# q and the gate operand transposed by DMA, x2 in row tiles of 128, column tiles and a new tail in an attention and convolution-gate kernel

## Chip, cores, metric

The kernel runs on one core of one Trainium2 chip. The metric is device time in microseconds (us) of one execution. A profile is one execution taken by the hardware profiler. Its engines are TensorE (PE for matmuls, PEld for weight loads), VectorE (DVE), ScalarE (ACT), GpSimd (POOL) and SyncE (SP), which in this kernel only issues DMAs. An eviction is the copy of a matmul result out of PSUM, where the matmuls of the kernel put it. A landing is the time from the issue of a DMA until its data have arrived.

## The reference

B = 8 batches, 8 heads, S = 576 positions, head width 64, model width DM = 512; all inputs fp32.

```python
# phi(x) = concat(relu(x)*cos, relu(x)*sin), cos and sin of pi/2 * position / S
q_p, k_p = phi(q), phi(k)
kv  = einsum('bhsf,bhsd->bhfd', k_p, v)
z   = sum(k_p, axis=s)
x   = einsum('bhsf,bhfd->bhsd', q_p, kv) / (einsum('bhsf,bhf->bhs', q_p, z) + 1e-6)
x   = heads side by side                                   # B, S, DM
x1, x2, x3 = split(x @ w_proj, 3)
x2_conv = irfft(rfft(x2, axis=s) * rfft(filter, axis=s))   # along the 576 positions
out = (x1 * x2_conv * x3) @ w_out                          # fp32
```

## The kernel before

One batch goes through `phi` (VectorE), `qt` (q transposed), `kv`, `num` and `att` (attention), `fx` (a fold of the positions that also transposes), `x2` and `dft` (forward transform), the gate (x1, x3, `g`), `inv` (inverse transform), `y` and `out`. Stages of three batches are interleaved by a scheduler. The parts that matter here, with cuts marked:

```python
qpt_buf = [consts.tile([128, NH, NT, 2, 64], FP16, ...) for i in range(1)]     # one buffer

def emit_qt(b, hp):                    # q is transposed by TensorE
    u = psum.tile([128, 2, 1024], FP16, ...)
    for hh in range(2):
        for j in range(NJ):
            nc.tensor.transpose(u[:, hh, ds(j * NP, NP)],
                                qp[:, j, 2 * hp + hh].rearrange("p a b -> p (a b)"), perm)
    ...                                # two evictions to qpt, VectorE and ScalarE

def emit_num(b, hp):
    ...                                # reads qpt as weights: the first reader of the transposed q

def emit_x2(b, bls):                   # 24 matmuls of 96 rows
    for bl in bls:
        for comp in range(2):
            for c in range(NC):
                nc.tensor.matmul(u[0:NP, comp], fx[:, c, ds(comp * 6 + 2 * bl, 2)]...,
                                 wp16[:, c, ds(DM, DM)], start=(c == 0), stop=(c == NC - 1))
        ...

OT = [0, 128, 256, 384, 448]
def emit_out(b, grps):
    ov = out[b].rearrange("(p j) n -> j p n", j=6)         # rows j, j+6, j+12, ... of the output
    for grp in grps:
        ...                                                # matmuls, eviction to os_
        for t in grp:
            ...                                            # pieces x..e of at most 96 rows
            src = os_[x - OT[t] : e - OT[t], t - grp[0]]
            dst = ov[jb, p_a:p_b]                          # 96 x 512: outermost count 96
            q_ = nc.scalar if b >= B - 2 and t % 2 == 1 else nc.sync
            q_.dma_start(out=dst, in_=src)
```

Of the kernel before, what the change touches and what calls it, by code (L numbers as in the profile page):

```python
# [17 lines left out]
def kernel(  # L18
# [15 lines left out]

    nc = tc.nc
# [6 lines left out]
    NT = 5  # L42
# [25 lines left out]
    tcol = consts.tile([128, NJ], FP32, tag="tcol", name="tcol")  # L68
    epsc = consts.tile([128, NT], FP32, tag="epsc", name="epsc")
    perm = consts.tile([NP, NP], FP16, tag="perm", name="perm")  # L70
# [5 lines left out]
    fm = consts.tile([128, 24, 10], FP16, tag="fm", name="fm")  # L76
    tre = consts.tile([NP, 3, NP], FP16, tag="tre", name="tre")
    tim = consts.tile([NP, 3, NP], FP16, tag="tim", name="tim")

# [9 lines left out]
    qpt_buf = [consts.tile([128, NH, NT, 2, 64], FP16, tag=f"qpt{i}", name=f"qpt{i}") for i in range(1)]  # L89
# [24 lines left out]
    raw_t = {}  # L114

    def load_qk(b, nm, hs=slice(0, NH)):
        src = {"q": q, "k": k, "v": v}[nm]
        if hs.start == 0:
            rw = work.tile([NP, NH, NJ * D], FP16, tag="raw", bufs=4, name=f"{nm}raw{b}")
            raw_t[(b, nm)] = rw  # L120
        nc.gpsimd.dma_start(
            out=raw_t[(b, nm)][:, hs], in_=src[b, hs].rearrange("h (p j) d -> p h (j d)", j=NJ)
        )

    def emit_va(b, xs=range(4)):
        for x in xs:
            hs = slice(2 * x, 2 * x + 2)
            nc.scalar.copy(  # L128
                out=va_buf[b % 2][:, hs, :, 0:D],
                in_=raw_t[(b, "v")][:, hs].rearrange("p h (j d) -> p h j d", j=NJ),  # L130
            )
# [28 lines left out]
    def emit_iotas(part):  # L160
# [13 lines left out]
        iota("sr_i", [NP, QS], lambda t: [(t, [[2, 3], [12, NP // 2]], 1, 0)])  # L174

    def emit_cols():
# [6 lines left out]
        nc.vector.memset(warm, 0.0)  # L183
        sj = cc["s6_i"]
# [3 lines left out]
        nc.vector.tensor_tensor(out=tcol, in0=tcol, in1=scol, op=AL.mult)  # L188

        u16 = small("u16p")  # L190
        rnd(u16, p, 1.0 / 16.0, -15.0 / 32.0)
        dest = small("dest")
        tsc(dest, p, 6.0, AL.mult)
        nc.vector.scalar_tensor_tensor(
            out=dest, in0=u16, scalar=-95.0, in1=dest, op0=AL.mult, op1=AL.add
        )
        tsc(perm, cc["nrow_i"], dest[0:NP], AL.is_equal)

    def emit_pads():
        for va in va_buf:  # L200
            nc.vector.memset(va[:, :, :, D : D + 2], 1.0 / A1)
        for t in qpt_buf:
            nc.vector.memset(t[:, :, :, 0, 60:64], 0.0)
            nc.vector.memset(t[:, :, :, 1, 0:4], 0.0)

    def emit_fm():

        p = cc["p"]
        loc = small("loc")
        side = small("side")  # L210
        nc.vector.tensor_copy(out=loc[0:64], in_=p[0:64])
        tsc(loc[64:128], p[64:128], -1.0, AL.mult, 127.0, AL.add)
        nc.vector.memset(side[0:64], 1.0)
        nc.vector.memset(side[64:128], -1.0)
        lo = small("lo")
        rnd(lo, loc, 1.0 / 6.0, -5.0 / 12.0)
        li = small("li")
        nc.vector.scalar_tensor_tensor(
            out=li, in0=lo, scalar=-6.0, in1=loc, op0=AL.mult, op1=AL.add
        )  # L220


        orb = small("orb", NT)
        for t in range(NT):
            tsc(orb[:, t : t + 1], lo, 10.0 * t, AL.add)
        oj = small("oj", NT)
        rnd(oj, orb, 1.0 / 16.0, -15.0 / 32.0)
        pos = small("pos", NT)

        tsc(pos, orb, 6.0, AL.mult)  # L230
        nc.vector.scalar_tensor_tensor(
            out=pos, in0=oj, scalar=-95.0, in1=pos, op0=AL.mult, op1=AL.add
        )
        nc.vector.scalar_tensor_tensor(
            out=pos, in0=li.to_broadcast([128, NT]), scalar=96.0, in1=pos, op0=AL.mult, op1=AL.add
        )
# [6 lines left out]
        orow_i = cc["orow_i"][:, 0:10]  # L243
        match = small("match", 10)
# [5 lines left out]
        for sl, (kk, c0) in enumerate([(0, 0.25), (3, 0.25), (1, 0.25), (1, 0.0), (2, 0.25), (2, 0.0)]):  # L250
# [4 lines left out]
        nc.scalar.activation(out=coef[:, 0:6], in_=ph, func=AF.Sin, scale=TWO_PI)  # L255
        tsc(coef[:, 3:6:2], coef[:, 3:6:2], 1.0 / R3, AL.mult)

        tsc(coef[:, 0:6], coef[:, 0:6], 2.0, AL.mult)
        tsc(coef[:, 0:6], coef[:, 0:6], RC, AL.add, -RC, AL.add)
        tsc(coef[:, 0:6], coef[:, 0:6], 0.5, AL.mult)  # L260
        tsc(coef[:, 6:12], coef[:, 0:6], side, AL.mult)
# [12 lines left out]
            in0=coef.unsqueeze(2).to_broadcast([128, 24, 10]),  # L274
            in1=match.unsqueeze(1).to_broadcast([128, 24, 10]),
# [23 lines left out]
    def emit_rows():  # L299
# [5 lines left out]
        par = cc["par"] = small("par")  # L305
        rnd(par, p, 0.5, -0.25)
        nc.vector.scalar_tensor_tensor(
            out=par, in0=par, scalar=-2.0, in1=p, op0=AL.mult, op1=AL.add
        )
# [10 lines left out]
    def emit_fwd_tables():  # L320
# [4 lines left out]
        u = small("u16")  # L325
        rnd(u, p, 1.0 / 16.0, -15.0 / 32.0)
        j = small("jr")
        nc.vector.scalar_tensor_tensor(
            out=j, in0=half, scalar=-3.0, in1=u, op0=AL.mult, op1=AL.add
        )  # L330
        w = small("w2s")

        tsc(w, p, 12.0, AL.mult, 1.0, AL.add)
        nc.vector.scalar_tensor_tensor(out=w, in0=u, scalar=-192.0, in1=w, op0=AL.mult, op1=AL.add)
        nc.vector.scalar_tensor_tensor(out=w, in0=j, scalar=2.0, in1=w, op0=AL.mult, op1=AL.add)
# [24 lines left out]
        for tb in (tre, tim):  # L360
            tsc(tb[:, 1:3], tb[:, 1:3], amp[0:NP], AL.mult)
            nc.vector.tensor_tensor(out=tb[:, 0], in0=tb[:, 0], in1=mask, op=AL.mult)

# [59 lines left out]
    def emit_h():  # L423
        hc, hs_, hb, alt = cc["hc"], cc["hs"], cc["hb"], cc["alt"]
        fa = filt16.rearrange("p x (j n) -> p x j n", j=3)
        for x, op in ((0, AL.add), (1, AL.subtract)):
# [5 lines left out]
        for bl in range(3):  # L432
# [15 lines left out]
            tsc(h3[:, bl, 1], u[0:NP, 1], sc, AL.mult)  # L448
            nc.vector.tensor_copy(out=h3[:, bl, 2], in_=h3[:, bl, 1])
        u = unit("h_nyq")  # L450
        for j in range(3):
            nc.tensor.matmul(
                u[0:1, 0], alt[:, j % 2 : j % 2 + 1], feo[:, 0, j], start=(j == 0), stop=(j == 2)
            )
        nc.scalar.activation(out=h3[0:1, 0, 2], in_=u[0:1, 0], func=AF.Copy, scale=1.0 / S)
# [4 lines left out]
    def emit_phi(b, nm, h0=0, nh=NH):  # L460
        rw = raw_t[(b, nm)]
        dst = kp_t if nm == "k" else qp_t
        if h0 == 0:
            dst[b] = work.tile([NP, NJ, NH, 2, D], FP16, tag=f"{nm}p", bufs=2 if nm == "q" else 1, name=f"{nm}p{b}")
        t = dst[b]
        if nm == "q":

            tsc(
                t[:, :, h0 : h0 + nh, 0],
                rw[:, h0 : h0 + nh].rearrange("p h (j d) -> p j h d", j=NJ), 0.0, AL.max,  # L470
            )
        for j in range(NJ):
            for cs, col in ((0, ccol), (1, scol)) if nm == "k" else ((1, tcol),):
                mark["phi", b, nm] = tsc(
                    t[:, j, h0 : h0 + nh, cs], rw[:, h0 : h0 + nh, ds(j * D, D)],
                    col[0:NP, j : j + 1], AL.mult, 0.0, AL.max,
                )
# [21 lines left out]
    def emit_qt(b, hp):  # L499
        qp, qpt = qp_t[b], qpt_buf[0]  # L500
        u = psum.tile([128, 2, 1024], FP16, tag="u", bufs=4, name=f"qt{b}_{hp}")
        for hh in range(2):
            for j in range(NJ):
                nc.tensor.transpose(  # L504
                    u[:, hh, ds(j * NP, NP)],
                    qp[:, j, 2 * hp + hh].rearrange("p a b -> p (a b)"),
                    perm,
                )
        hsl = slice(2 * hp, 2 * hp + 2)
        ev = nc.scalar.copy if b == 0 and hp < 2 else nc.vector.tensor_copy  # L510
        mark["qpt", b, hp] = ev(  # L511
            out=qpt[:, hsl, :, 0, 0:60],
            in_=u[:, :, 0:300].rearrange("p h (t c) -> p h t c", c=60),
        )
        nc.scalar.copy(  # L515
            out=qpt[:, hsl, ::-1, 1, 4:64],
            in_=u[:, :, 276:576].rearrange("p h (t c) -> p h t c", c=60),
        )

    def emit_num(b, hp, wm=0):  # L520
        qpt, kvs = qpt_buf[0], kvs_t[b]
        if hp == 0:
            att_t[b] = work.tile([128, NT, DM], FP16, tag="att", bufs=2, name=f"att{b}")
# [3 lines left out]
        for hh in range(2):  # L527
            h = 2 * hp + hh
            for t in range(NT):
                nc.tensor.matmul(  # L530
                    u[:, hh, ds(t * 65, 65)], qpt[:, h, t].rearrange("p a b -> p (a b)"),
                    kvs[:, h // 4, ds((h % 4) * 65, 65)], start=True, stop=True,
                )
        nv = u[:, :, 0 : NT * 65].rearrange("p h (t e) -> p h t e", e=65)
        rcp = work.tile([128, 2, NT], FP32, tag="rcp", bufs=2, name=f"rcp{b}_{hp}")
        nc.vector.tensor_tensor(
            out=rcp, in0=nv[:, :, :, 64], in1=epsc.unsqueeze(1).to_broadcast([128, 2, NT]), op=AL.add
# [5 lines left out]
            in1=rcp.unsqueeze(3).to_broadcast([128, 2, NT, D]),  # L543
# [3 lines left out]
    def emit_fx(b, cs=range(NC), ccs=None, wm=0):  # L547
        att = att_t[b]
        if 0 in cs:
            fx_t[b] = work.tile([128, NC, 24, 48], FP16, tag="fx", bufs=2, name=f"fx{b}")  # L550
        fx = fx_t[b]
        for c in cs:
            u = unit(f"fx{b}_{c}")
            warm_up(u, wm)
            for t in range(NT - 1):
                nc.tensor.matmul(  # L556
                    u[:, t // 2, 0:480].rearrange("p (g o) -> p g o", o=20)[:, :, ds((t % 2) * 10, 10)],
                    att[:, t, ds(c * 128, 128)], fm, start=True, stop=True,
                )
            nc.scalar.copy(  # L560
# [319 lines left out]
```

## Time and profile before

| | before |
|---|---|
| time, median of 3 runs | 270.46 us (270.35 to 270.78) |
| TensorE busy | 243.0 us, 90% of the span |
| steady period per batch | 28.5 us, of it TensorE 27.9 |
| last 13.6 us | output evictions wait for stores |

The prediction below shows and reads the main views. Two lines more: TensorE's busy share in 40 slices of the span (each digit in tenths), and the issue line of the large output stores, whose last number is the median from issue to landing.

```profile
PE   0287998878989999999999999999999999999991
...
out_dram<-os SPq DMA_DIRECT2D x22, 192.0 KB, 2.5
```

Each digit is the mean busy share of the core's 16 DMA engines in 0.3 us.

```profile
DMA  0000000000289899965891039956779453799971
```

### The profile page before, as it was taken

To read this page: it belongs to the slowest core of one execution; us is meant where nothing else is said; L and a number is where in the kernel's file an instruction comes from. 1 tells how busy PE (TensorE), PEld (TensorE's weight loads), DVE (VectorE), ACT (ScalarE), POOL (GpSimd) and SP (SyncE) were. 2 spreads that over 40 slices of the span, in tenths; PEclk is the share of its full clock that TensorE was granted. 3 is DMA by queue.
4 is the path that set the end of the run, shared out by engine and by line. 5 is a ranking of instruction groups with operands and counts; after the bars stand their busy time and mean duration, and the time that the engine had idled before them with its cause. 6 is when DMAs were issued, how large, how long until landed. Compare 5 with 4: busy or idle time off the path is not lost.

```text
span 271.2 us, 6320 instructions
## 1 busy us (share of the span) xinstructions
PE 243.0 (90%) x2457; PEld 175.2 (65%) x2457; DVE 226.9 (84%) x805; ACT 196.8 (73%) x274; POOL 27.3 (10%) x47
## 2 busy tenths in 40 slices
PE   0287998878989999999999999999999999999991
PEld 0164767547858776786678676867687768756830
DVE  7689997998899898979897989978997479646951
ACT  2279679798497778877897789786977667857630
POOL 8551111020020101110111011000000000000000
PEclk9999999995799999999999999999999999999998
DMA  5999998919019296636860868114000600060235
GB/s 79 168 206 205 206 205 122 166 14 169 3 14 161 33 230 90 89 40 152 150 101 3 174 128 124 16 51 125 0 2 9 169 2 0 2 174 13 69 117 155
DMA packets 26991, 26.70 MB, mean 98 GB/s; under 512 B 1680, under 2 KB 22160, under 8 KB 26960
## 3 DMA queue, kind: packets, MB, share of 16 engines
q0 software_dynamic: 21200, 16.84, 42.7%
q1 hardware_dynamic: 5120, 8.39, 10.7%
q10 hardware_dynamic: 640, 1.05, 1.3%
q8 instruction: 19, 0.31, 0.5%
q14 instruction: 12, 0.10, 0.1%
HBM read 33.69 MB, written 9.44 MB: 159 GB/s over the span
## 4 chain that ended last, share of the span: by engine, by line
PE 50%; ACT 22%; DVE 21%; DMA 4%; issue 1%; POOL 0%; SPq 0%; POOLq 0%; ACTq 0%
PE x L630 20%; PE x L593 9%; ACT x2f L598 7%; ACT va L128 7%; PE kv L491 5%; PE out L695 4%; PE fx L556 4%; DVE eo L672 4%; ACT fx L560 3%; DMA vraw<-in_v_dram 2%; DVE kp L99 2%; PE qt L504 2%; PE dft L607 2%; PE inv L657 2%; DVE qpt L511 2%; PE inv L656 2%
## 5 line engine op out<-in xcount | busy, mean ns | idle before, releaser
L630 PE MATMUL x<-fx,wp 128*128 128x288 f16 x512 | 67.5, 286 | 1.1 <-ACT fx L560 1.0
L630 PEld LDWEIGHTS <-wp 128*128 128x128 f16 x512 | 50.0, 98 | 13.3 <-issue 0.3
L593 PE MATMUL x<-wp,fx 128*96 128x512 f16 x192 | 45.2, 382 | 0.5 <-ACT x2f L598 0.5
L560 ACT CAST fx<-fx 128x960 f16<-128x960 f32 x32 | 30.6, 961 | 13.7 <-PE fx L556 13.7
L695 PE MATMUL out<-wo,y 128*128 128x512 f16 x160 | 37.6, 379 | 0.7 <-DVE y L677 0.7
L598 ACT ACTIVATE x2f<-x 96x1024 f16<-96x1024 f32 x24 | 24.5, 1020 | 14.6 <-PE x L593 14.6
L593 PEld LDWEIGHTS <-fx 128*96 128x96 f16 x192 | 22.4, 124 | 15.1 <-issue 0.8
L672 DVE TENSOR_TENSOR eo<-eq 128x144 f16<-128x144 f16 x128 | 23.7, 228 | 10.1 <-ACT eq L660 9.9
L128 ACT COPY va<-vraw 96x768 f16<-96x768 f16 x32 | 25.3, 827 | 9.3 <-DMA vraw<-in_v_dram 9.3
L638 DVE TENSOR_TENSOR g<-x,x1s 128x288 f16<-128x288 f32 x64 | 27.0, 448 | 1.3 <-PE x L630 1.1
L491 PE MATMUL kv<-va,kp 96*128 96x65 f16 x384 | 16.4, 202 | 11.7 <-ACT va L128 8.8
L540 DVE TENSOR_TENSOR att<-num,rcp 128x640 f16<-128x640 f32 x32 | 26.1, 820 | 0.3
L515 ACT COPY qpt<-qt 128x600 f16<-128x600 f16 x32 | 20.4, 671 | 7.5 <-DVE qpt L511 7.5
L695 PEld LDWEIGHTS <-y 128*128 128x128 f16 x160 | 14.9, 97 | 16.0 <-DVE y L677 1.2
L609 ACT CAST xf<-dft 96x1024 f16<-96x1024 f32 x24 | 23.5, 1010 | 2.2 <-PE dft L607 1.2
L491 PEld LDWEIGHTS <-kp 96*128 96x128 f16 x384 | 15.3, 104 | 13.3 <-DVE kp L99 8.1
L504 PEld LDWEIGHTS <-qp 96*128 96x128 f16 x384 | 20.2, 102 | 5.1 <-issue 1.1
L636 ACT CAST x1s<-x 128x576 f16<-128x576 f32 x32 | 20.5, 639 | 4.2 <-PE x L630 3.1
L612 DVE TENSOR_TENSOR m<-xf,h 96x1024 f16<-96x1024 f16 x24 | 16.3, 678 | 7.8 <-ACT xf L609 7.7
L504 PE MATMUL qt<-perm,qp 96*128 96x96 f16 x384 | 21.7, 213 | 0.5 <-ACT fx L560 0.3
L700 ACT ACTIVATE os<-out 128x1024 f32<-128x1024 f32 (+1 forms) x21 | 18.3, 883 | 5.2 <-PE out L695 5.1
L556 PE MATMUL fx<-fm,att 128*128 128x240 f16 x128 | 18.8, 270 | 2.2 <-DVE att L540 1.1
(185 smaller groups left out, 419.4 us busy)
## 6 DMA issues: line engine op xcount, KB each, us to landing
out_dram<-os SPq DMA_DIRECT2D x22, 192.0 KB, 2.5
qraw<-in_q_dram POOLq DMA_DIRECT2D x7, 576.0 KB, 6.6
kraw<-in_k_dram POOLq DMA_DIRECT2D x7, 576.0 KB, 6.3
vraw<-in_v_dram POOLq DMA_DIRECT2D x7, 576.0 KB, 6.5
out_dram<-os SPq DMA_DIRECT2D x20, 128.0 KB, 2.4
wp<-in_moe_w_proj_dram POOLq DMA_DIRECT2D x3, 512.0 KB, 12.3
out_dram<-os SPq DMA_DIRECT2D x22, 64.0 KB, 2.1
kraw<-in_k_dram POOLq DMA_DIRECT2D x2, 288.0 KB, 6.4
```

Of the source, the lines that this page charges most:

```text
L128: nc.scalar.copy(out=va_buf[b % 2][:, hs, :, 0:D], in_=raw_t[(b, "v")][:, hs].rearrange("p h (j d) -> p h j d", j=NJ),)
L491: nc.tensor.matmul(u[:, h // 4, ds((h % 4) * 65, 65)], kp[:, j, h].rearrange("p a b -> p (a b)"), va[:, h, j, 0:65], start=(j == 0), stop= ...
L504: nc.tensor.transpose(u[:, hh, ds(j * NP, NP)], qp[:, j, 2 * hp + hh].rearrange("p a b -> p (a b)"), perm,)
L540: mark["att", b, hp] = nc.vector.tensor_tensor(out=att[:, :, ds(hp * 128, 128)].rearrange("p t (h d) -> p h t d", h=2), in0=nv[:, :, :, 0: ...
L556: nc.tensor.matmul(u[:, t // 2, 0:480].rearrange("p (g o) -> p g o", o=20)[:, :, ds((t % 2) * 10, 10)], att[:, t, ds(c * 128, 128)], fm, s ...
L560: nc.scalar.copy(out=fx[:, c, :, 0:40].rearrange("p g (u o) -> p u g o", u=2), in_=u[:, :, 0:480].rearrange("p u (g o) -> p u g o", o=20),)
L593: nc.tensor.matmul(u[0:NP, comp], fx[:, c, ds(comp * 6 + 2 * bl, 2)].rearrange("p a b -> p (a b)"), wp16[:, c, ds(DM, DM)], start=(c == 0) ...
L598: mark["x2f", b, bl] = nc.scalar.mul(out=x2f[:, bl], in_=u[0:NP], mul=X2SC)
L630: nc.tensor.matmul(u[:, hf, 0:HS], wp16[:, i, ds(w * DM + c * 128, 128)], fx[:, i, ds(12 + 6 * hf, 6)].rearrange("p a b -> p (a b)"), star ...
L638: mark["g", b, c] = nc.vector.tensor_tensor(out=(g[:, c, 0:HS] if hf == 0 else g[:, c, HS:S][:, ::-1]).rearrange("p (j i o) -> p j i o", j ...
L672: nc.vector.tensor_tensor(out=eoh[:, a, :, ds(48 * x, 48)], in0=eqj[:, a, 0], in1=eqj[:, a, 1], op=op)
L695: nc.tensor.matmul(u[:, x], y[:, c, ds(OT[t], 128)], wo16[:, c], start=(c == 0), stop=(c == NC - 1),)
```

## The change

The intent: take work off TensorE, the fullest engine. q is transposed by DMA from batch 2 on; the gate operand is transposed by DMA for the last three batches instead of folded on TensorE; x2 uses full row tiles of 128, with zero-padded DFT tables to take up the shifted rows; a last tile of 64 columns goes through two column tiles; the tail is rearranged. To suit the new order of positions (pairs of blocks side by side) the output rows get a new view too. The core of the diff, with cuts marked:

```diff
+    XT_DMA = (5, 6, 7)
+    DMA_QT = 2
...                                            # emit_qt
+        if b >= DMA_QT:
+            nc.sync.dma_start_transpose(
+                out=qpt[:, hsl].rearrange("p h (j n) -> p (h j) n", j=NJ),
+                in_=qp[:, hsl].rearrange("p h j a b -> p (h j a b)"),
+            )
+            return
...                                            # emit_xt, for batches in XT_DMA
+        nc.sync.dma_start_transpose(
+            out=xt_t[b].rearrange("p t c n -> p (t c) n"),
+            in_=att_t[b].rearrange("p t n -> p (t n)"),
+        )
...                                            # emit_x2: 16 matmuls of 128 rows, then
+                for c in range(2):
+                    for x in range(2):
+                        mm(u[ds(64 * x, 64), 0], 4, 64, c + 2 * x, range(2 * x, 2 * x + 2))
...                                            # emit_gate: x3 through ScalarE to fp16
+            nc.scalar.copy(out=x3s, in_=us[1][:, :, 0:HS])
...                                            # emit_out
-    OT = [0, 128, 256, 384, 448]
+    OT = [0, 128, 256, 384, 512]
-        ov = out[b].rearrange("(p j) n -> j p n", j=6)
+        ov = out[b].rearrange("(k x y) n -> x y k n", x=2, y=6)
...
-                    dst = ov[jb, p_a:p_b]
-                    q_ = nc.scalar if b >= B - 2 and t % 2 == 1 else nc.sync
-                    q_.dma_start(out=dst, in_=src)
+                    m, k0 = pos // 48, pos % 48
+                    e = pos + 96 if pos % 96 == 0 and pos + 96 <= hi_ else min(hi_, (m + 1) * 48)
+                    q_ = nc.sync
+                    if last:
+                        q_ = (nc.sync, nc.scalar)[store[0] % 2]
+                    ...
+                    if e - pos == 96:
+                        q_.dma_start(out=ov[:, m // 2], in_=sv[pos - OT[t] : e - OT[t]])
+                    elif t < 4 or last:
+                        q_.dma_start(out=ov[m % 2, m // 2, k0 : k0 + e - pos], in_=...)
```

## The prediction

> **What bounds the kernel now.** I read the page first (busy time, slices), then the busy time by stage, then TensorE's timeline of one steady batch, then VectorE's, then the waits of the tail.
>
> ```profile
> PE 243.0 (90%) x2457; PEld 175.2 (65%) x2457; DVE 226.9 (84%) x805; ACT 196.8 (73%) x274; POOL 27.3 (10%) x47
> ...
> PEclk9999999995799999999999999999999999999998
> DMA  5999998919019296636860868114000600060235
> ```
>
> ```profile
> 50.00:71.40 21.40, 18.12 (x203) 14.00 (x202) 20.22 (x64) 16.23 (x23) 1.54 (x2) 0.77 0.64 94
> ...
> 129.30:157.80 28.50, 27.89 (x303) 20.66 (x302) 25.68 (x85) 23.03 (x31) 2.32 (x3) 1.00 0.63 113
> 157.80:186.30 28.50, 27.89 (x303) 20.67 (x302) 25.68 (x85) 23.04 (x31) 1.54 (x2) 1.00 0.46 85
> ```
>
> The columns of the stage table are span, then busy us of PE, PEld, DVE, ACT, POOL, then clock, DMA share and GB/s. After some 71 us of set-up the kernel repeats a period of 28.5 us per batch, in which TensorE is busy 27.9 us: it is the bound. VectorE (25.7) is close behind, ScalarE (23.0) less so. In the set-up VectorE is the full one, and from 61 to 71 us TensorE runs at about half clock.
>
> ```profile
> 133.81 1.90 PE L593 MATMUL x<-wp,fx 128*96 128x512 f16 x8
> ...
> 136.86 0.38 PE L607 MATMUL dft<-x2f,tre 96*96 96x512 f16 x1 [0.28 <-ACT x2f L598]
> 137.08 0.38 PE L607 MATMUL dft<-x2f,tim 96*96 96x512 f16 x1
> 137.29 2.12 PE L630 MATMUL x<-fx,wp 128*128 128x288 f16 x16
> 139.25 0.57 PE L556 MATMUL fx<-fm,att 128*128 128x240 f16 x4
> 139.66 2.12 PE L630 MATMUL x<-fx,wp 128*128 128x288 f16 x16
> ...
> 151.46 1.89 PE L695 MATMUL out<-wo,y 128*128 128x512 f16 x8
> 153.19 0.68 PE L504 MATMUL qt<-perm,qp 96*128 96x96 f16 x12
> 153.70 1.03 PE L695 MATMUL out<-wo,y 128*128 128x512 f16 x4
> ```
>
> A printed mean (286 ns for a gate matmul) is latency; what an instruction costs is the distance from start to start. From this timeline: x2 217 ns, dft 215, gate 122 (16 in 1.96 us), fx 102, its remainder fxc 82, out 215, qt 42.5 (12 in 0.51), and in the same way num 30.5, kv 32, inv 65. It is close to the number of moving columns over 2.4 per ns, whatever the height. A batch: x2 24x0.217=5.2, num 40x0.0305=1.2, dft 6x0.215=1.3, gate 64x0.1225=7.8, fx and fxc 2.0, inv 2.1, out 20x0.215=4.3, qt 48x0.0425=2.0, kv 1.5: 27.5 of the 28.5 us.
>
> ```profile
> ACT os L702 <- DMA out_dram<-os: 3.1, 2, 2.0
> DVE os L97 <- ACT os L702: 2.8, 1, 2.8
> ACT os L700 <- PE out L695: 2.0, 1, 2.0
> DVE os L97 <- DMA out_dram<-os: 1.9, 1, 1.9
> ```
>
> These are the waits of the last 13.6 us (257.6 to the end): the last output tiles wait for stores to free their buffers, two DMA landings of about 2 us in a row on the path.
>
> **What the Trainium skill says.** "DMA: Bandwidth & Descriptors", section "Latency and other measured facts", gives 261 GB/s for a DMA transpose with a non-contiguous middle dimension. The trace of before has no such transpose and can't confirm it. "TensorEngine Tiling (Array Packing)", section "Key Properties": different tiles of the array execute in parallel, and a change of tiling mode drains the array. Before has no 64-column tile, so this is untried here too. "VectorE: DVE Perf Modes", section "Walkthrough: the 8-slice pipeline in each mode": two 16-bit values per cycle need 16-bit operands of step one; fp32 or PSUM operands fall back to one. The trace agrees: 128x288 takes 448 ns with an fp32 PSUM operand (g) and 304 ns all in fp16 (y<-eo). "TensorE: Matmul & The Clock Gate", Part 1: idle windows halve TensorE's clock. It agrees: 0.50 to 0.57 from 61 to 72 us, after a stretch with gaps; inv spacing there is 120 ns instead of 65.
>
> **The change, part by part** (counts from the changed kernel's instruction lists).
>
> q transposes: the short title speaks of the gate operand, but in the code q is also transposed by DMA from batch 2 on, four DMAs a batch. Removed: 6 batches x 2.04 = 12.2 us of TensorE, and four evictions each on VectorE and ScalarE per batch.
>
> Gate operand: fx and xt are now separate folds of 24 matmuls of 96 columns each (0.0425 us, from qt's equal width): 2.04 a batch against 1.97, so +0.6 over all. For the last three batches the xt half goes: 3x1.02 = -3.1.
>
> x2: 16 matmuls of 128 rows plus four 64-column tiles. 3.5 + (0.43 if tile pairs overlap, 0.87 if not) = 3.9 to 4.3 against 5.2: -7 to -10.5 over 8 batches. In exchange dft has 9 matmuls, not 6: +0.65x8 = +5.2. num has 48, not 40: +0.24x8 = +1.9.
>
> out: the fifth tile is 64 rows in two column tiles of 256 columns: 0.43 to 0.86 against 0.86: 0 to -3 over seven batches.
>
> TensorE sum: -12.2 +0.6 -3.1 -7..-10.5 +5.2 +1.9 +0..-3 = -14.6 to -21, say -18. A steady batch with the tensor fold is then 24.7 to 25.6 us of matmul, with the DMA gate 23.7 to 24.6.
>
> VectorE per steady batch, by distances: g from 0.365 to 0.22 because x3 is copied to fp16 by ScalarE, 8x0.145=-1.2; eo 16x0.145 to 8x0.22 = -0.6; qpt 4x0.38 = -1.5; two va copies taken over from ScalarE +0.8; att with six tiles +0.5: 25.7 to about 23.8. ScalarE: +4x0.56 for x3, +0.4 for the folds, -4x0.57 qpt, -2x0.72 va, -0.4 x2f: about 21.5, and 19 with the DMA gate. Neither passes TensorE, though VectorE comes within 2 us of it.
>
> DMA: the share of 0.63 in a 28.5 us stage is 18 us. Four transposes of 96x1536 fp16 (295 KB) at the page's rate are 1.13 us each, 4.5 a batch (an estimate from that page), and q's load in halves makes more, smaller packets, perhaps +1.5. That is 24 of some 26 us: nearly full. The author's stopping at three batches for the gate operand fits this: the three last are those with the least input still to load. Since qp is made one batch ahead, a batch's transposes have about 20 us from the last read of qpt by num to their use, so latency is hidden.
>
> Tail: five single buffers instead of shared ones, evictions split over two engines, the last contraction step held back until y is whole. The two landings in a row go: from the last gate matmul to the end I expect 9.5 us (y 2.5, output matmuls 3.5, evict 0.5, issue and landing 3) instead of 13.6: -4.
>
> Set-up: x2(0) fills gaps of the set-up, so the half-clock stretch may shrink (inv's 32 matmuls lost 1.8 us and kv 1 there), but VectorE is full there and gains only about 1.5: 0 to -3.
>
> Sum: 270.5 -18 -4 -1.5 = 247. I don't take all of it: where TensorE, VectorE and ScalarE are all near 90% a period ends later than its fullest engine, today by 1 us of wait. Adding 0.6 us in each of five periods gives 250.
>
> **The rivals.**
> A. VectorE takes over. It waits 2.8 us a period today (1.8 of it for the first eq). If it keeps those waits, a period is 23.8+2.8=26.6, only 1.9 less than now; five periods give -9.5, with tail, set-up and last batches about 256. For: 84% busy over the span, against 90%. Also in the gate stage ScalarE needs 4x0.57=2.3 us per column block against TensorE's 2.5, so PSUM is freed just in time. Against: only this stage is tight for ScalarE.
> B. The transposes are several times slower than the page's rate. At 3.4 us each the DMA need is 18+1.5+13.6=33 us a batch, above the period; num would wait for qpt, stores queue behind them on the same issuing engine, and the time would be 270 to 280. For: no transpose in the trace to go by, one issuing queue. Against: the author kept four a batch and added three more.
> C. Everything is realised, tile pairs overlap and the clock dip vanishes: 242 to 244.
>
> **Range and chances.** The main sum gives 250, A 256, C 243. I centre on 250 with 241 to 260, which leaves B and worse outside. B with more than half its loss is what it takes to be within 2% or slower: faster 0.92, same 0.06, slower 0.02.
>
> **What would show it.** Right: the steady period is 25.5 to 26.5 us with TensorE still over 93% busy in it; no qt matmul after batch 1; g at about 300 ns and eo about 300; 64-column x2 tiles in pairs that start within a few ns or 217 ns apart (settles 0.43 or 0.87); DMA share near 0.9 in the middle; 9 to 10 us from last gate matmul to end, without a wait of an eviction for a store. Wrong: transposes that take over 3 us of all engines, with waits of num for qpt; VectorE without idle time while TensorE waits for g, att or y; a set-up longer than 72 us before x2 of batch 1 is done.

## The result

| | before | after |
|---|---|---|
| median | 270.4 us (270.17 to 270.78, 4 runs) | 280.87 us (279.63 to 281.85, 4 runs) |
| ratio to before | | 1.038 (95% 1.034 to 1.043): slower |
| TensorE busy | 243.0 us | 230.5 us |
| mean granted clock, profiled run | 0.978 | 0.929 |

A ratio here and below is the mean time of one kernel's fast runs over that of the other's of the same rounds, so not quite the ratio of the medians quoted. The prediction of 250 us (241 to 260) was wrong, in direction too.

TensorE did get less to do. The page's slices (TensorE, its granted clock, the DMA engines) show where the time is lost instead: in slices 22 to 24, a little at 28, at 36 and in the last three, where before was full but for the last.

```profile
PE   0379979989699999999993559998999999959600
...
PEclk9995999998999999999997579999999999988965
DMA  6999997999991978998959989897989493232330
```

The busy time by stage (columns as in the prediction) shows a period as predicted, then (one undisturbed period is left out) the disturbed one, then 14.7 us at the end in which TensorE does nothing:

```profile
95.40:120.69 25.29, 25.29 (x295) 18.16 (x293) 24.31 (x77) 20.96 (x32) 3.54 (x5) 1.00 0.92 121
...
145.98:185.00 39.02, 28.38 (x268) 18.37 (x267) 22.85 (x72) 19.20 (x28) 1.54 (x2) 0.83 1.17 141
264.40:279.10 14.70, 0.00 (x0) 0.00 (x0) 0.00 (x0) 0.38 (x1) 0.00 (x0) 0.57 0.21 54
```

The first line is what the prediction asked for: 25.29 us a period, TensorE without a gap. The chain of work that ended last, in order of time (start, us, what), names the two losses: landings of transposed q in the middle, landings of stores near the end.

```profile
144.34 1.63 PE kv L543 x48
...
146.21 17.29 DMA qpt<-qp
163.54 0.57 PE num L584 x12
...
184.01 7.21 DMA qpt<-qp
...
231.72 7.12 DMA out_dram<-os
238.86 0.62 SPq L842
239.53 8.13 DMA out_dram<-os
```

A landing on the chain is not idle time in full, since TensorE can have other work meanwhile: in the period of the first one it is idle for 10.6 us (39.02 - 28.38). The waits of `num` for q (in total, times, longest), to be compared with those of the experiments; the kernel has a second such line, of PE instead of PEld, with 11.4 us:

```profile
PEld L584 <- DMA qpt<-qp: 13.8, 5, 4.5
```

SyncE's timeline ahead of the first loss (start, us, queue, line): six stores are issued at 130.2 to 135.4 us, then the four transposes of q, and issuing these four takes 24 us.

```profile
130.16 0.62 SPq L842 DMA_DIRECT2D out_dram<-os  x1
130.83 2.40 SPq L844 DMA_DIRECT2D out_dram<-os  x1
133.35 2.01 SPq L849 DMA_DIRECT2D out_dram<-os  x4
135.47 24.01 SPq L555 DMA_TRANSPOSE qpt<-qp  x4
```

Line 842 is the new 96-row store, the one with an outermost count of 2. Now the DMA view of the end, 267.5 to 276.5 us, to be held against that of before, from 258 to 270 us:

```profile
DMA  1111112021011111111111111111111111111111
...
q1 hardware_dynamic: 110, 0.22, 7.3%
q10 hardware_dynamic: 106, 0.20, 5.9%
```

Nothing else competes there, only the last stores, and yet the 16 engines are busy by one tenth: 7.3 + 5.9 = 13.2% of 16 engines is 2.1 engines. The packet records say the same: nearly always two packets of 2 KB are in flight (in over 90% of the time, mostly three in the rest), and 216 packets go in 9 us, 11 of them of a few bytes. So a 96-row store of 96 packets occupies two engines for about 96 / 24 = 4 us (an estimate from these numbers), and two of them in the two queues take 8 us, as the chain's 7.12 and 8.13 show; a store of the same size landed in 2.5 us before. From 139 to 142 us the records show two store packets active while 19 packets of 256 bytes of the transposes are in flight without progress.

The records show the middle in two steps. From 137.8 to 144.2 us no packet of a transpose completes. No packet of a two-engine store is in flight after 143 us and until the next store is issued at 159.6, yet the four transposes end only at 164.2, at some 200 packets per us: by then loads share the engines, at about 180 packets per us. In e1 below the same four transposes have the engines to themselves and take 6.7 us (131.65 to 138.39), some 680 packets per us. So the stores' delay also moved the transposes into the time of the loads; no run separates the two parts. The page's DMA share doesn't show the standstill, as packets that stand still count as busy: slices 20 and 21 have 9 and 5 tenths, but only 81 and 51 GB/s.

This agrees with the Trainium skill, "DMA: Bandwidth & Descriptors", section "Why a DMA increments its semaphore by 16 and not by 1", paragraph "How many engines (k)": the number of engines is the largest number up to 16 that divides the slowest dimension of both access patterns. For 96 rows that is 16; for 2 x 48 it is 2.

**Theory S** (stores): the two-engine stores cause the loss, in the middle because the transposes are held up with them, at the end because the last stores are slow themselves. **Theory V** (volume; the prediction's rival B): the transposes are too much for the DMA engines, and the stores merely queue behind them.

### The profile page after: what moved, and what is told of

Read it like the earlier page. It is cut to its first block, busy times and chain, and to the rows that moved or that the text cites. A ratio compares the mean times of both kernels' runs of the same rounds, so it can differ in the third digit from the quotient of the medians.

```text
span 279.1 us, 6336 instructions
## 1 busy us (share of the span) xinstructions
PE 230.5 (83%) x2405; PEld 158.6 (57%) x2405; DVE 213.3 (76%) x747; ACT 184.3 (66%) x287; POOL 35.9 (13%) x61
## 4 chain that ended last, share of the span: by engine, by line
PE 60%; DMA 16%; ACT 10%; DVE 5%; issue 1%; ACTq 1%; POOL 0%; SPq 0%; POOLq 0%
PE x L713 21%; DMA qpt<-qp 9%; PE out L785 8%; PE x L648 7%; DMA out_dram<-os 5%; PE fx L611 4%; PE dft L680 4%; PE kv L543 3%; PE num L584 3%; PE inv L749 3%; PE inv L750 3%; ACT va L145 2%; DMA vraw<-in_v_dram 2%; DVE att L594 2%; PE qt L563 1%; PE out L803 1%
## 5 line engine op out<-in xcount | busy, mean ns | idle before, releaser
L713 PE MATMUL x<-xt,wp 128*128 128x288 f16 x512 | 67.9, 287 | 3.4 <-ACT os L829 3.4
L666 ACT ACTIVATE x2f<-x 128x1024 f16<-128x1024 f32 (+1 forms) x24 | 21.2, 884 | 30.5 <-PE x L648 30.5
L648 PE MATMUL x<-wp,fx 128*128 128x512 f16 (+1 forms) x160 | 39.0, 410 | 2.1 <-DVE qpt L569 1.6
L594 DVE TENSOR_TENSOR att<-num,rcp 96x768 f16<-96x768 f32 x32 | 30.4, 949 | 0.4
L785 PE MATMUL out<-wo,y 128*128 128x512 f16 (+1 forms) x132 | 30.2, 379 | 0.0
L584 PE MATMUL num<-kvs,qpt 128*128 128x65 f16 (+1 forms) x384 | 18.7, 205 | 13.2 <-DMA qpt<-qp 11.4
L723 ACT CAST x3s<-x 128x576 f16<-128x576 f32 x32 | 20.5, 641 | 6.7 <-PE x L713 6.4
L626 ACT CAST fx<-fx 128x576 f16<-128x576 f32 x32 | 20.6, 643 | 5.1 <-PE fx L611 5.1
L611 PE MATMUL fx<-fm,att 96*128 96x96 f16 x312 | 19.9, 210 | 2.9 <-DVE att L594 1.1
L543 PEld LDWEIGHTS <-kp 96*128 96x128 f16 x384 | 14.6, 101 | 12.4 <-DVE kp L107 8.0
L764 DVE TENSOR_TENSOR eo<-eq 128x288 f16<-128x288 f16 x64 | 17.7, 299 | 4.4 <-ACT eq L753 4.3
L785 PEld LDWEIGHTS <-y 128*128 128x128 f16 (+1 forms) x132 | 12.5, 98 | 14.6 <-issue 1.0
## 6 DMA issues: line engine op xcount, KB each, us to landing
kraw<-in_k_dram POOLq DMA_DIRECT2D x7, 576.0 KB, 10.6
```

What stands on the lines that cost most here:

```text
L543: nc.tensor.matmul(u[:, h // 4, ds((h % 4) * 65, 65)], kp[:, j, h].rearrange("p a b -> p (a b)"), va[:, h, j, 0:65], start=(j == 0), stop= ...
L584: nc.tensor.matmul(u[0:m, hh, ds(t * 65, 65)], qpt[:, c0 : c0 + 2 * m - 1 : 2], kvs[:, h // 4, ds((h % 4) * 65, 65)], start=True, stop=True,)
L594: mark["att", b, hp] = nc.vector.tensor_tensor(out=att[:, :, ds(hp * 128, 128)].rearrange("p t (h d) -> p h t d", h=2), in0=nv[:, :, :, 0: ...
L611: nc.tensor.matmul(dst.rearrange("p (g e o) -> p g e o", e=2, o=8)[:, :, e], att[:, 2 * j + e, ds(c * 128, 128)], fm[0:NP, gs], start=True ...
L626: mark["fx", b] = nc.scalar.copy(out=dst[:, c].rearrange("p g (j o) -> p j g o", j=3), in_=uf[:, 0:768].rearrange("p (j g o) -> p j g o", ...
L648: nc.tensor.matmul(dst, fx[:, c].rearrange("p g o -> p (g o)")[:, ds(128 * ch, n)], wp16[:, c, ds(DM, DM)], start=(c == cs[0]), stop=(c == ...
```

## The experiments

All were timed in three rounds beside the kernel before, and unless said otherwise edit the changed kernel. Medians of before were 270.4 to 270.5 us. Medians and ranges in the table are of all four runs, ratios of the fast ones. Two of the four runs of e5 were slow ones, and one each of e9 and e10; the medians of their fast runs are 293.1, 296.7 and 268.6 us, and the text below compares these.

| run | edit | median us (range) | ratio to before |
|---|---|---|---|
| e1_split_stores | 96-row stores as two of 48 | 250.43 (249.74 to 250.9) | 0.925 |
| e2_q_by_pe | q by TensorE | 287.73 (285.42 to 288.59) | 1.062 |
| e3_gate_by_pe | gate operand by TensorE | 283.6 (281.52 to 284.72) | 1.047 |
| e4_split_q_by_pe | e1 and e2 | 270.44 (269.67 to 272.01) | 1.000 |
| e5_stores_on_act | 96-row stores from ScalarE's queue | 297.99 (292.37 to 304.57) | 1.085 |
| e6_before_two_engines | before, stores with an outer count of 2 | 288.95 (288.02 to 292.0) | 1.073 |
| e7_split_gate5 | e1, gate by DMA in five batches | 247.36 (244.9 to 248.29) | 0.914 |
| e8_split_gate6 | e1, gate by DMA in six batches | 244.45 (242.85 to 245.46) | 0.904 |
| e9_split_2x24 | e1's stores, each as 2 x 24 | 297.81 (295.5 to 304.87) | 1.100 |
| e10_split_last_two | e1 in the last two batches only | 269.65 (267.17 to 273.72) | 0.995 |
| e11_split_first_six | e1 in the first six batches only | 261.52 (261.17 to 262.42) | 0.967 |

### e1_split_stores: the stores alone

```diff
-  e = pos + 96 if pos % 96 == 0 and pos + 96 <= hi_ else min(hi_, (m + 1) * 48)
+  e = min(hi_, (m + 1) * 48)
```

Each 2 x 48 store becomes two plain stores of 48 rows; bytes, rows and queue stay.

> Edit: only the output stores change; a store of 96 rows whose HBM side is an array of 2 x 48 rows is cut in two stores of 48 rows. Theory S (two-engine stores): a store with 2 as its outermost count runs on two DMA engines only (in the trace of the changed kernel exactly two 2 KB packets are in flight for the last 9 us), and the transposes that stand behind it in the same queue stall with it. Then the waits of num for qpt (17.3 and 7.2 us on the path), the store waits near the end and the 14 us after the last eviction all go: 242 to 254 us, no wait of num for qpt over 2 us. Theory V (volume of 256-byte transpose packets fills the DMA engines): nothing but the tail changes, 268 to 282 us, and num still waits for qpt by 15 us or more.

Measured: 250.43 us, correct, ratio 0.9253 (0.9214 to 0.9293). Volume is untouched and the loss is gone: V falls as the cause. The slices of TensorE, and the stages of a batch with the gate folded and of one with the gate by DMA:

```profile
PE   0197897998988999999999999999999999999990
```

```profile
121.14:146.42 25.28, 25.28 (x294) 18.16 (x293) 23.56 (x75) 20.96 (x32) 3.55 (x5) 1.00 0.94 166
146.42:170.63 24.21, 24.21 (x271) 17.09 (x269) 22.49 (x72) 19.16 (x28) 1.54 (x2) 1.00 1.16 189
```

The DMA share passes 1 because packets overlap in time: up to 31 are in flight on the 16 engines. SyncE issues the four transposes of the same batch in 6.4 us instead of 24, and the DMA view of the last stores (240 to 247 us) is high again:

```profile
130.46 6.36 SPq L555 DMA_TRANSPOSE qpt<-qp  x4
```

```profile
DMA  0144278969899798667794869999996410000000
```

From issue to landing a transpose now takes 4.4 us in the median, against 7.0 in the changed kernel.

### e9_split_2x24: count of engines, or length of a store?

e1 also made the stores shorter. Here each of its 48-row stores is written as 2 x 24. The rows land in the wrong order, so the result is wrong; number and size of the stores are e1's.

```diff
-  q_.dma_start(out=ov[m % 2, m // 2, k0 : k0 + e - pos], in_=...)
+  dst = ov[m % 2, m // 2, k0 : k0 + e - pos]
+  if e - pos == 48:
+      dst = dst.rearrange("(k h) n -> h k n", h=2)
+  q_.dma_start(out=dst, in_=...)
```

> Edit: the split stores, but each 48-row store given a 2 x 24 form with its rows in another order (result wrong on purpose). Same number, size and place of the stores as in the split-store kernel; only the outermost count is 2 again. If the engine count that follows from that 2 is the cause, the loss is back: 275 to 292 us. If it was the length of a store or the splitting as such: 249 to 253 us.

Measured: 296.7 us in the fast runs, above the expected range and 46 us more than e1. That it is worse than the changed kernel fits eight stores with 384 rows a batch through two engines here, where the changed kernel has three with 288. The outer count of 2 does it, not the length. Its waits (in total, times, longest) grow in both places:

```profile
PEld L584 <- DMA qpt<-qp: 18.7, 6, 6.7
...
ACT os L829 <- DMA out_dram<-os: 14.3, 3, 6.1
```

### e6_before_two_engines: the store form in the kernel before

```diff
  dst = ov[jb, p_a:p_b]
+ if e - x == NP:
+     dst = dst.rearrange("(k x) n -> x k n", x=2)
```

Rows are again in the wrong order.

> Edit: the kernel before, its 96-row stores given a 2 x 48 form with rows in another order (result wrong on purpose, same bytes, same number of stores). No transposes by DMA here. If the slow form alone costs time: 96-row stores land in 6 us or more instead of 2.5, the buffer waits of the tail grow, total 273 to 283 us, steady periods 28.5 us unchanged. If the form is harmless without transposes: 269 to 272 us.

Measured: 288.95 us, ratio 1.0729; the loss of 18.5 us is larger than expected. It lies at the end: TensorE is idle in the last three slices, and three middle stages have the period of before. One of them, the same to 0.01 us:

```profile
153.25:181.75 28.50, 27.89 (x303) 20.67 (x303) 25.68 (x84) 23.03 (x32) 1.54 (x2) 1.00 0.50 85
```

So the same slow stores hurt in the middle only where transposes share the engines and queue with them. An estimate fits, which takes the DMA share for the need of each engine (too high, as packets overlap): three stores of 4 us on two engines ask for 12 us of them a batch, where spread over 16 they ask for about 1.5. Before's stages have a DMA share of 0.46 to 0.63, so 13 to 18 us of each engine in a period of 28.5; with 10.5 more the two engines stay within 28.5. In e1's 25.3 us the share is 0.84 to 0.94, or 21 to 24 us; with 10.5 more they would need 32 to 34.

### e10 and e11: how much is middle, how much is end

```diff
   # e10_split_last_two: slow stores stay in batches 0 to 5
-  e = pos + 96 if pos % 96 == 0 and pos + 96 <= hi_ else ...
+  e = pos + 96 if pos % 96 == 0 and pos + 96 <= hi_ and b < B - 2 else ...
   # e11_split_first_six: slow stores stay in batches 6 and 7
+  e = pos + 96 if pos % 96 == 0 and pos + 96 <= hi_ and b >= B - 2 else ...
```

> Edit: the changed kernel with the stores of only the last two batches split. The end loses its waits (17 to 18 us, which the slow form cost where no q transpose was near), the stalls of num in the middle stay: 261 to 267 us. If the stalls of the middle only moved the end, 250 to 256 or 278 to 282.

> Edit: the changed kernel with the stores of all batches but the last two split. The middle runs freely, num doesn't wait for qpt, the end pays for the slow stores: 263 to 270 us.

Measured: 268.6 us in the fast runs of e10, a little above its expected range, and 261.52 us for e11, a little below. e10 keeps the wait of `num`, e11 loses only the end (the slices of TensorE):

```profile
PEld L584 <- DMA qpt<-qp: 13.7, 5, 4.9
```

```profile
PE   0298897998969999999999999999999999999200
```

Against e1's 250.43 the middle costs 18.2 us and the end 11.1, together 29.3; the changed kernel is 30.4 above e1. The two losses add up to within 1.1 us, less than the range of e10's fast runs (267.17 to 270.65).

### e2, e3, e4: what the transposes are worth

```diff
   # e2_q_by_pe, and e4_split_q_by_pe together with e1's edit
-  DMA_QT = 2
+  DMA_QT = 8
   # e3_gate_by_pe
-  XT_DMA = (5, 6, 7)
+  XT_DMA = ()
```

> Edit: q transposed by TensorE in all batches, stores and gate as in the changed kernel. Theory V: without the 24 q transposes the DMA has room; a period is 25.3 + 2.0 = 27.3 us, the stalls of num go, about 258 to 264 us. Theory S: the two-engine stores still hold back the gate transposes and the tail, 266 to 274 us, with the 8 to 9 us of two packets in flight still at the end.

> Edit: gate operand folded by TensorE in all batches, q by DMA and stores as in the changed kernel. Both theories: the first stall (17.3 us, before any gate transpose) stays. S: 275 to 285 us. V: six transposes' worth of 30 less, so 270 to 277 us.

> Edit: the split stores and q by TensorE together. Both theories: no stall, period 27.3 us; 254 to 260 us. If S holds it is slower than the split stores alone by about 5 to 10 us (6 x 2.04 us of TensorE work come back); if V holds it is faster than the split stores alone.

Measured: e2 at 287.73 us missed what both theories expected. Without q transposes there is no wait of `num` for a DMA, yet the slow stores remain at the end: the pair e2 and e4, which differ only in the stores, are 17.3 us apart. e3 at 283.6 lies in S's range: no gate transpose is left in it, and the loss stays.

e4 was expected at 254 to 260 and came to 270.44, no better than before. All other parts of the change together gain nothing without the q transposes by DMA, and these are worth 20 us (270.44 - 250.43), not the 12.2 us of TensorE time that the prediction had counted for them. Its stages show why:

```profile
132.60:160.80 28.20, 27.57 (x343) 20.36 (x341) 25.05 (x78) 23.23 (x36) 2.28 (x4) 1.00 0.58 105
```

The period is 28.2 us against e1's 25.28 at the same place: 2.3 us of TensorE (2.04 was counted for the 48 matmuls), and 0.6 us of waits. VectorE and ScalarE have the evictions back (25.05 and 23.23 us busy instead of 23.56 and 20.96); that this makes the waits is likely, but not shown. Where e1 already has the gate by DMA a period of e4 is 27.8 against 24.21, with 1.3 us of waits. The remaining difference, to 20 us, I didn't settle; e4's chain of work runs through VectorE's `kp` and `att`.

### e5_stores_on_act: order in the queue, or the engines themselves?

```diff
-  q_ = nc.sync
+  q_ = nc.scalar if e - pos == 96 else nc.sync
```

The slow stores leave the transposes' queue, but stay on two engines. If only order in the queue hurt, this would help.

> Edit: in the changed kernel every 96-row store keeps its 2 x 48 form (two engines) but is issued from ScalarE's queue instead of SyncE's, where the transposes are. Theory S1 (order in the queue: a transpose waits only because the slow store stands before it in the same queue): num no longer waits for qpt, the middle runs at 25.3 us a period, and only the tail stays slow: 254 to 264 us. Theory S2 (occupancy: two engines have about 13 us of stores a batch beside 12 us of loads and 8 us of transposes, more than a 25 us period, whatever queue they come from): num still waits for qpt by 8 us or more: 268 to 285 us.

Measured: 292.37 and 293.81 us in the two fast runs, slower still than the changed kernel, so neither range was right. The profiled run was a slow one; it is read here only for order and packets. ScalarE itself was now held up (two stores took it 10.7 us to issue, and its `kvs` evictions waited for 21 us, by the profile for landings of transposes), so the move added a wait of its own, and the time doesn't decide.

The packet records say a part. `num` still waits for q: a landing of 18.5 us stands on the chain. But the standstill is gone: from 131 to 137 us, with the slow stores' packets in flight from ScalarE's queue, transposes complete at some 120 packets per us beside the stores and loads, and at 628 when alone (151 to 158 us). So standing behind the stores in a queue is not all of it; how much of the slowness is the stores' and how much the loads' stays open.

### e7 and e8: a version that beats both

```diff
   # with e1's edit
-  XT_DMA = (5, 6, 7)
+  XT_DMA = (3, 4, 5, 6, 7)        # e7_split_gate5
+  XT_DMA = (2, 3, 4, 5, 6, 7)     # e8_split_gate6
```

> Edit: split stores, and the gate operand by DMA in five batches (3 to 7) instead of three. Two more batches save 1.02 us each of TensorE: 248 to 249 us if the DMA engines have room; if the share of 0.94 in batch 3's period means they are full, waits of num or gate for a transpose and 250 to 256 us.

> Edit: split stores, and the gate operand by DMA in six batches (2 to 7). With room: 247 to 248 us. Without: 250 to 258 us.

Measured: 247.36 and 244.45 us, both correct. e8 is the fastest version, 9.6% below before (ratio 0.9039, 0.8985 to 0.9094); the ranges of e7 and e8 touch between 244.9 and 245.5, so their order is likely, not certain. With the stores mended there was room for more transposes than the change had used. Little may be left: e8's chain carries one landing of q again. Of its 11.3 us TensorE was idle for about 1.1; it had other work meanwhile.

```profile
136.56 11.34 DMA qpt<-qp
```

## Why the prediction was wrong, step by step

**The step that failed** is the one that was not taken: the form of the stores. The DMA step counted the transposes' bytes and the smaller packets of q's load, and took the stores to be as before: the new outermost count of 2, and the two engines that follow from it, are in no term. From there it said "a batch's transposes have about 20 us from the last read of qpt by num to their use, so latency is hidden", and of the tail "The two landings in a row go". Both were false in the changed kernel: one landing of a transpose takes 17.3 us of the chain, and the end has two landings in a row of 7.1 and 8.1 us in place of two of 2. e1 shows that the first step holds once the stores use 16 engines (`num` has no wait for a transpose), and the second nearly: one landing of 2.3 us stays on the chain before the last eviction. e10 and e11 give what each was worth: 18.2 and 11.1 us.

**The rest of the sum held, in part by luck.** e1 has every part of the change but the store form, and takes 250.43 us where 250 was predicted. The terms below held one by one, but what they are worth in time did not: q was worth 20 us by e4 against e1, the other parts together nothing by e4 against before, where about 12 and 8 had been counted. Either two errors cancel or the parts help one another; no run tells which.
- TensorE: 243.0 us busy before, 223.0 in e1, so -20.0 where -14.6 to -21 was worked out and -18 taken.
- The period was to be 24.7 to 25.6 us with the tensor fold and 23.7 to 24.6 with the DMA gate: 25.3 and 24.2. The prediction's addition of 0.6 us of wait a period was not needed; TensorE is busy for the whole of these stages.
- VectorE was to need about 23.8 us, ScalarE 21.5 and 19: 23.6 to 24.3, and 20.96 and 19.16 in the stages of e1 and the changed kernel.
- Column tiles: the four 64-column matmuls of x2 take 0.55 us, nearer the 0.43 of overlapping pairs than 0.87. The two of a pair start 4 ns apart, the sign that the prediction had named.
- The tail: 9.5 us were expected from the last gate matmul to the end; e1 takes 11.1 (236.9 to 248.0). The landing named above and three stores more to issue may be part of it; no run separates this.

**A term mis-sized without harm:** a transpose of 295 KB was put at 1.13 us of all engines, from the page's 261 GB/s. In e1 the two hardware queues took 35.6% and 0.8% of 248 us, 90.3 us; before, without transposes, 10.7% and 1.3% of 271, 32.5 us. The difference of 58 us over 30 such transposes (24 for q, three of twice the size for the gate) is 1.9 us each, an estimate that takes the stores' share as unchanged and counts overlapping packets in full. The four transposes that ran alone in e1 took 6.7 us, so 1.7 us each, 175 GB/s. The DMA engines still had room for it.

**Rival B** had the symptoms right (`num` waiting for qpt, stores and transposes in one queue, 270 to 280 us, where 280.87 was measured) and got the cause wrong: it needed 3.4 us a transpose. The chance given to slower, 0.02, rested on volume being the only way for DMA to fail.

**The q transposes were undervalued:** 12.2 us by TensorE's time alone, 20 by e4 against e1. They also relieve two engines that were nearly full, which is the likely reason, not a shown one.

## What to carry to other kernels

When a change rewrites the view of a tensor in a DMA, read the outermost count of both sides, not only bytes and the contiguous run: a count of 2 put a 192 KB store on two DMA engines here and cost 30 us of 250. Slow stores can be harmless for as long as nothing shares their engines and queue; look at what a change puts there, and at the end of the kernel where nothing hides them. The sign to look for is a DMA system that moves few bytes while the kernel waits for landings. Read the GB/s and not the busy share alone: the share was low at the end of this kernel, but high in the middle, where packets stood still.

## What the Trainium skill lacked or had wrong

- "DMA: Bandwidth & Descriptors", section "Why a DMA increments its semaphore by 16 and not by 1": its rule for the number of engines is right (two packets in flight, 13.2% of 16 engines, for 2 x 48 rows), and "Rules for kernel authors" on the page repeats it as an advice to use all 16 engines. What the page lacks is a measured time of a transfer on few engines and its effect on the transfers beside it. Here: a 192 KB store in about 4 us of two engines alone, two such stores in 7 to 8 us, against a landing of 2.5 us on 16, and transposes landing after 7.0 us in the median instead of 4.4.
- The same page, section "Latency and other measured facts": it gives 261 GB/s for a transpose with a non-contiguous middle dimension, with no shape or packet size; e1 shows 175 GB/s for SBUF to SBUF transposes of 96 x 1536 fp16 in 256-byte packets, with nothing beside them. Whether this transpose is the page's case isn't shown.
- "TensorEngine Tiling (Array Packing)", section "Key Properties": that tiles run in parallel is confirmed, but no cost is given for a change of tiling mode; x2's pairs of 64-column tiles took 0.55 us where 0.43 would be two full overlaps. Whether the 0.12 us are that cost isn't shown.
